# Chunk 0's decays by broadcast from DRAM, the loads reordered, decode 1 to 4 in block 0's first product

## The chip, the cores and the metric

The kernel runs on one core of one Trainium2 chip. The time is device microseconds of that core from one launch; a run's figure is the median of several executions.

## What is computed

Two stages follow each other. The first is a Mamba-2 recurrence over 4 batches and 8 heads (32 pairs), 768 tokens, head size 32 and state size 16. With cum the running sum of log(a) inside a chunk, L[i, j] = exp(cum[i] - cum[j]) for j up to i and zero elsewhere, a chunk gives

```
y     = ((C B^T) * L) x  +  (C state) * exp(cum)
state = exp(cum[last]) * state + sum_j B_j x_j exp(cum[last] - cum[j])
```

The second stage is a dense layer pair on the 3072 x 256 result: h = y @ w_in (256 x 2048), g = h * clip(h + 3, 0, 6) / 6, out = g @ w_out (2048 x 256). The two weights arrive as 64-bit floats; the kernel turns their bits into 32-bit floats itself.

## The kernel before, in words

The reference takes chunks of 32 tokens; the kernel takes chunks of P = 128, so NC = 6 chunks c for each of NB = 4 batches b. Block k of the dense stage holds chunk k of all four batches (512 tokens). The order of all work is written out by hand: each engine runs its instructions in the order in which the program names them, and SP's queue issues its DMAs in that order too.

**Decays.** a is loaded first; clip, Ln and a scan on DVE (lines 192 to 195) give cum for all 32 (b, h) rows. Four DMAs on ScalarE's queue (line 200) write it to DRAM as cum_d. For chunks 1 to 5, `load_decay` (line 205) reads a 4 KB row of cum_d into all 128 partitions (512 KB for each batch), `decay` (line 272) masks it on POOL (for c over 1 it also adds cum_n there) and takes the exponential on ScalarE. `load_eto` (line 212) fetches the rows that scale C for the state term, by eight DMAs. For chunk 0 the kernel builds the differences on TensorE instead: `diff_first` (line 220) puts the mask into a PSUM tile with one matmul and adds each head's row with four more, twice for each batch, and `decay_first` (line 235) takes the exponentials out of PSUM.

**One chunk.** `ends` scales B and, after chunk 0, the old state. `turn` transposes C and B of two batches. `scores` makes C B^T for the heads in four PSUM tiles and multiplies them into L on DVE. `mix` makes y and the state's part; `keep` copies y to yT (ScalarE) and the state (DVE). For chunks from 1 on these pieces come from the generator `steps` (line 426), which yields between them so that they can be set among the dense matmuls of the block before.

**Dense stage.** `mlp_in(k, f)` makes a 128 x 512 tile h for each of 16 values of f (two products of a k half each), then r on ScalarE and gT on DVE. `mlp_out(k, b, f0, f1)` sums over f into the output of batch b. The PSUM pool `ps` has four tiles shared by h, t_ps and cb.

**Weights.** Each weight matrix has four pieces of 1 MB: pieces 0 to 3 are w_in (four f each), 4 to 7 are w_out (four f each). `load_w(i)` loads a piece into one of three raw buffers; `decode_a`, `decode_b`, `decode_c` turn it into fp32. decode_a: the top 16 bits copied on ScalarE; mantissa, exponent and sign cut on DVE; the exponent rebased by a Relu on ScalarE (line 163), with bias bias_e. decode_b: clamp the exponent and add the sign (line 169), join the low mantissa bits (line 171), and start the load of piece i + 3. decode_c: the product (line 185).

**The hand-written order.** Lines 110 to 113 issue w piece 0, chunk 0's C, B and x, then w pieces 1 and 2. Lines 457 to 488 do chunk 0 with decodes 0 and 1 set among its parts, then the loads of chunk 1. From line 491 on a table `weave` spreads decodes 2 to 5 over the 16 f of block 0's first product, three parts in three of four f; decode 6 stands ahead of block 0's second product and decode 7 inside it. `next(todo)` after f 9, after f 13 and later advances the following chunk.

Of the kernel before, what the change touches and what calls it, by code (L numbers as in the profile page):

```python
# [8 lines left out]
FP32 = mybir.dt.float32  # L9
U32 = mybir.dt.uint32  # L10
U16 = mybir.dt.uint16
BF16 = mybir.dt.bfloat16
AF = mybir.ActivationFunctionType
ALU = mybir.AluOpType
# [5 lines left out]
def kernel(  # L20
# [48 lines left out]
    def big(shape, name):  # L69

        return att.tile(shape, FP32, name=name, tag="big", bufs=8)
# [5 lines left out]

    loaded = {}

    def load(c):  # L80
        sl = slice(c * P, (c + 1) * P)
        bc = loads.tile([P, 2, NB * NH, N], FP32, name="bc")
        xt = loads.tile([P, NB * NH, D], FP32, name="xt")
        for j, src in enumerate((C, B)):
            nc.sync.dma_start(  # L85
                out=bc[:, j], in_=src[:, :, sl, :].rearrange("b h s n -> s (b h) n"))
        nc.sync.dma_start(out=xt, in_=x[:, :, sl, :].rearrange("b h s d -> s (b h) d"))
        loaded[c] = bc, xt

    w_in = const.tile([P, NK, DF], FP32, name="w_in")  # L90
    w_out = const.tile([P, NF, DM], FP32, name="w_out")
# [5 lines left out]
    def load_w(i):  # L97
        raw = loads.tile([P, NK * FP * 2 * P], U32, name="raw", bufs=NRAW)
        if i < NP:
            cols = slice(2 * i * FP * P, 2 * (i + 1) * FP * P)  # L100
            src = moe_w_in[:, cols].rearrange("(k p) f -> p k f", p=P)
            dst = raw.rearrange("p (k f) -> p k f", k=NK)
        else:
            r0 = (i - NP) * FP * P
            src = moe_w_out[r0:r0 + FP * P, :].rearrange("(k p) m -> p k m", p=P)
            dst = raw.rearrange("p (k m) -> p k m", k=FP)
        nc.sync.dma_start(out=dst, in_=src)
        raws[i] = raw

    load_w(0)  # L110
    load(0)
    load_w(1)
    load_w(2)
    nc.scalar.preload_act_table_set("natural_log_exp_and_others")


    ident = const.tile([P, P], FP32, name="ident")
    make_identity(nc, ident)
    ident_h = const.tile([P, P], BF16, name="ident_h")
    nc.vector.tensor_copy(ident_h, ident)  # L120
    hide = const.tile([P, P], BF16, name="hide")
    nc.gpsimd.memset(hide, 0.0)
    nc.gpsimd.affine_select(
        out=hide, in_=hide, pattern=[[1, P]], compare_op=ALU.is_ge,
        fill=-1e5, base=0, channel_multiplier=-1)
    run = big([NB * NH, NC, P], "run")
    nc.vector.memset(run, 1.0)
    nc.vector.memset(run[:, :, 0:1], 0.0)
    half = const.tile([P, 1], FP32, name="half")
    nc.vector.memset(half, 0.5)  # L130
    bias_e = const.tile([P, 1], FP32, name="bias_e")
    nc.vector.memset(bias_e, -896.0 * 2 ** 7)
    head = const.tile([P, 2, HU, D], FP32, name="head")
    nc.gpsimd.memset(head, 1.0)
    nc.gpsimd.affine_select(
# [9 lines left out]
    def decode_a(i):  # L145

        n = NK * FP * P
        top = raws[i].bitcast(U16).rearrange("p (n w) -> p n w", w=4)[:, :, 3]  # L150
        hi = raws[i].rearrange("p (n w) -> p n w", w=2)[:, :, 1]
        s = att.tile([P, n], U16, name="ws")
        e = att.tile([P, n], U16, name="we")
        m = att.tile([P, n], U32, name="wm")
        nc.scalar.copy(out=s, in_=top)
        nc.vector.tensor_scalar(
            out=m, in0=hi, scalar1=0xFFFFF, scalar2=0x100000,
            op0=ALU.bitwise_and, op1=ALU.bitwise_or)
        nc.vector.tensor_scalar(  # L159
            out=e, in0=s, scalar1=0x7FF0, scalar2=None, op0=ALU.bitwise_and)  # L160
        nc.vector.tensor_scalar(
            out=s, in0=s, scalar1=0x8000, scalar2=None, op0=ALU.bitwise_and)
        nc.scalar.activation(e.bitcast(BF16), e, AF.Relu, bias=bias_e, scale=8.0)  # L163
        halves[i] = s, e, m

    def decode_b(i):
        s, e, m = halves[i]
        lo = raws.pop(i).rearrange("p (n w) -> p n w", w=2)[:, :, 0]
        nc.vector.scalar_tensor_tensor(
            out=e, in0=e.bitcast(BF16), scalar=255.0 * 2 ** 7, in1=s, op0=ALU.min, op1=ALU.add)  # L170
        nc.vector.scalar_tensor_tensor(
            out=m.bitcast(FP32), in0=lo, scalar=2.0 ** -32, in1=m, op0=ALU.mult, op1=ALU.add)
        if i + NRAW < 2 * NP:
            load_w(i + NRAW)

    def decode_c(i):
# [18 lines left out]
    nc.vector.tensor_tensor_scan(  # L195
        out=flat, data0=run.rearrange("g c p -> g (c p)"), data1=a_sb, initial=0.0,
        op0=ALU.mult, op1=ALU.add)
    cum_d = dram.tile([NB, NC, NH, P], FP32, name="cum_d")
    for b in range(NB):
        nc.scalar.dma_start(  # L200
            out=cum_d[b].rearrange("c h p -> h c p"), in_=cum[b * NH:(b + 1) * NH])

    Ls, etos, diffs = {}, {}, {}

    def load_decay(c, b, queue):
        L = big([P, NH, P], "L")
        src = cum_d[b, c].rearrange("h p -> (h p)").unsqueeze(0)
        queue.dma_start(
            out=L.rearrange("j h i -> j (h i)"), in_=src.to_broadcast([P, NH * P]))
        Ls[c, b] = L  # L210

    def load_eto(c):
        eto = att.tile([P, NB, P], FP32, name="eto")
        for h in range(NH):
            nc.sync.dma_start(  # L215
                out=eto[h * N:(h + 1) * N],
                in_=cum_d[:, c, h].unsqueeze(0).to_broadcast([N, NB, P]))
        etos[c] = eto

    def diff_first(b):  # L220

        rows = NB * NH
        for u in range(2):
            g = b * NH + HU * u
            d = ps_o.tile([P, HU, P], FP32, name="d", tag="o")
            nc.tensor.matmul(
                out=d, lhsT=ident_h, rhs=hide.unsqueeze(1).to_broadcast([P, HU, P]),
                start=True, stop=True)
            for q in range(HU):
                nc.tensor.matmul(  # L230
                    out=d[:, q], lhsT=ident[:rows, g + q:g + q + 1].to_broadcast([rows, P]),
                    rhs=cum[:, 0], start=False, stop=True, skip_group_check=True)
            diffs[b, u] = d

    def decay_first(b):
        Ls[0, b] = big([P, NH, P], "L")
        for u in range(2):
            decay_exp(0, b, diffs.pop((b, u)), HU * u, HU)

    def decay_exp(c, b, src, h0, n):  # L240

# [184 lines left out]
    def steps(c):  # L426

        ends(c)
        turn(c, 0)
        decay(c, 0)  # L430
        yield
        turn(c, 1)
        decay(c, 1)
        yield
        for b in range(NB):
            scores(c, b)
            if c + 1 < NC:
                load_decay(c + 1, b, nc.sync)
            if b + 2 < NB:
                decay(c, b + 2)  # L440
            if b:
                mix(c, b - 1)
            if b == 2:
                keep(c, 0)
            yield
        mix(c, 3)
        keep(c, 1)
        if c + 1 < NC:
            load_eto(c + 1)

    def decode(i):
        decode_a(i)
        decode_b(i)
        decode_c(i)


    decode_a(0)
    by_token()
    diff_first(0)
    turn(0, 0)  # L460
    decay_first(0)
    turn(0, 1)
    decode_b(0)
    decode_c(0)
    ends(0)
    diff_first(1)
    scores(0, 0)
    decay_first(1)
    decode_a(1)
    diff_first(2)  # L470
    scores(0, 1)
    mix(0, 0)
    decay_first(2)
    decode_b(1)
    diff_first(3)
    scores(0, 2)
    mix(0, 1)
    keep(0, 0)
    decay_first(3)
    decode_c(1)  # L480
    scores(0, 3)
    mix(0, 2)
    mix(0, 3)
    keep(0, 1)
    load(1)
    load_eto(1)
    for b in range(NB):
        load_decay(1, b, nc.sync)


    weave = {}
    for i in range(2, 6):
        for j, part in enumerate((decode_a, decode_b, decode_c)):
            weave[0, 4 * (i - 2) + j] = part, i
    for k in range(NC):
        todo = steps(k + 1) if k + 1 < NC else iter(())
        for f in range(NF):
            mlp_in(k, f)
            if (k, f) in weave:
                part, i = weave[k, f]  # L500
                part(i)
            if f in (9, 13):
                next(todo, None)
        if k + 2 < NC:
            load(k + 2)
        next(todo, None)
        if k == 0:
            decode(6)
            for i in range(NP):
                for b in range(2):  # L510
                    mlp_out(0, b, i * FP, (i + 1) * FP)
                if i == 1:
                    decode(7)
                if i != 0:
                    next(todo, None)
        else:
            for b in range(2):
                mlp_out(k, b, 0, NF)
                next(todo, None)
            mlp_out(k, 2, 0, NF // 4)  # L520
            next(todo, None)
            mlp_out(k, 2, NF // 4, NF)
        if k == 0:
            mlp_out(k, 2, 0, NF)
        next(todo, None)
        mlp_out(k, 3, 0, NF)
# [30 lines left out]
```

## Time and profile before

| Quantity | Value |
|---|---|
| Time, median of 3 runs | 457.46 us (456.75 to 457.71) |
| Profiled execution's own time | 457.29 us |
| Span in its profile | 455.6 us |
| PE busy | 425.9 us (93%) |
| DVE busy | 162.1 us (36%) |
| ACT busy | 139.0 us (31%) |
| POOL busy | 66.2 us (15%) |
| Mean granted TensorE clock | 0.984 |
| Data moved by DMA | 30.15 MB |

Busy time is the time in which an engine had an instruction under way. Matmuls are pipelined, so a busy PE is not one at its peak. The chain that ended last is followed back from the last instruction to what released it; a windows view gives the busy time of every engine in a stretch of the span. In a timeline row the first two numbers are start and duration, and the bracket tells the idle time before and who ended it. "issue" stands for time in which nothing that the profile shows was waited for. PE is TensorE's matmuls, PEld its weight loads, DVE VectorE, ACT ScalarE, POOL GpSimd, SP the engine that issues most DMAs.

### The profile page before, as it was taken

The numbers are of one execution on the slowest core, as the hardware profiler recorded it, in microseconds if no ns is written. First come the engines' busy times: TensorE is split into PE (matmuls) and PEld (weight loads), VectorE is DVE, ScalarE is ACT, GpSimd is POOL, SyncE is SP. The second block draws the span as 40 slices with busy tenths as digits, with TensorE's granted clock in tenths as the row PEclk, the third lists the DMA queues.
The fourth block names the chain that finished last, engine by engine and source line by source line (L and its number), as shares of the span: only waits on it lengthen the run. The fifth ranks groups of instructions, "written<-read, shape, count | busy, mean of one in ns | idle before, by whom it ended". The sixth has DMA issues, their size and how long they took to land.

```text
span 455.6 us, 5119 instructions
## 1 busy us (share of the span) xinstructions
PE 425.9 (93%) x2020; PEld 271.7 (60%) x2020; DVE 162.1 (36%) x289; ACT 139.0 (31%) x260; POOL 66.2 (15%) x59
## 2 busy tenths in 40 slices
PE   0899987799999999999899999899999999999997
PEld 0676432377864377854377854387854487744785
DVE  3266587884014432124422124413024512034100
ACT  2352546741024520024510024610035410143200
POOL 2000006000000920000910001923300000000000
PEclk9999998779999999999999999999999999999999
DMA  9928993930266003276013185013100000000000
GB/s 156 230 94 127 113 292 128 150 92 24 72 67 93 1 29 100 66 71 86 0 50 101 47 73 79 0 58 105 31 16 1 1 12 14 14 11 0 0 24 23
DMA packets 87048, 30.15 MB, mean 66 GB/s; under 512 B 75536, under 2 KB 81360, under 8 KB 87024
## 3 DMA queue, kind: packets, MB, share of 16 engines
q1 hardware_dynamic: 86800, 29.73, 34.3%
q8 instruction: 16, 0.26, 0.2%
q10 hardware_dynamic: 224, 0.10, 0.2%
q14 instruction: 8, 0.07, 0.1%
HBM read 26.57 MB, written 3.24 MB: 65 GB/s over the span
## 4 chain that ended last, share of the span: by engine, by line
PE 66%; issue 14%; SPq 5%; DVE 5%; ACT 3%; POOL 3%; DMA 3%; ACTq 0%; POOLq 0%
PE o L417 35%; PE h L403 18%; PE cb L335 3%; SPq L215 3%; PE d L230 3%; PE y L364 2%; DVE gT L409 2%; PE y L358 2%; DMA eto<-cum_d 1%; ACT r L408 1%; POOL L L277 1%; SPq L85 1%; POOL L L278 1%; PE y L370 1%; PE t_ps L313 1%
## 5 line engine op out<-in xcount | busy, mean ns | idle before, releaser
L403 PE MATMUL h<-yT,w_in 128*128 128x512 f32 x384 | 171.2, 602 | 4.9 <-DVE csT L325 3.1
L417 PE MATMUL o<-w_out,gT 128*128 128x256 f32 x768 | 175.2, 386 | 0.0
L417 PEld LDWEIGHTS o<-w_out,gT 128*128 128x128 f32 x768 | 145.7, 192 | 25.2 <-issue 6.0
L403 PEld LDWEIGHTS h<-yT,w_in 128*128 128x128 f32 x384 | 72.7, 193 | 92.3 <-issue 83.7
L409 DVE SCALAR_TENSOR_TENSOR gT<-r,h 128x512 f32<-128x512 f32 x96 | 64.9, 686 | 133.3 <-ACT r L408 133.3
L408 ACT ACTIVATE r<-h,half 128x512 f32<-128x512 f32 x96 | 64.0, 685 | 70.9 <-PE h L403 70.9
L343 DVE TENSOR_TENSOR L<-L,cb 128x256 f32<-128x256 f32 x96 | 34.0, 416 | 78.8 <-PE cb L335 76.1
L422 ACT COPY ob<-o 128x256 f32<-128x256 f32 x24 | 8.9, 372 | 165.8 <-PE o L417 133.1
L277 POOL TENSOR_TENSOR L<-L,cum_n 128x1024 f32<-128x1024 f32 x16 | 30.3, 1895 | 14.9 <-DMA L<-cum_d 14.9
L301 POOL TENSOR_TENSOR tmp<-state,eto 128x512 f32<-128x512 f32 x4 | 4.2, 1046 | 188.1 <-ACT eto L298 188.1
L335 PE MATMUL cb<-cT,bT 32*128 32x256 f32 x192 | 25.1, 474 | 6.2 <-DVE gT L409 4.7
L278 POOL TENSOR_SCALAR_AFFINE_SELECT L<-L 128x1024 f32<-128x1024 f32 x20 | 23.7, 1189 | 1.2
L335 PEld LDWEIGHTS cb<-cT,bT 32*128 32x128 f32 x192 | 11.2, 205 | 17.9 <-DVE gT L409 9.9
L282 ACT ACTIVATE L<-L 128x1024 f32<-128x1024 f32 x16 | 17.0, 1063 | 11.8 <-POOL L L278 11.8
L364 PE MATMUL y<-L,xt 128*32 128x128 f32 x384 | 17.3, 297 | 0.0
L230 PEld LDWEIGHTS d<-cum,ident 32*128 32x128 f32 x64 | 14.2, 323 | 4.5 <-issue 4.5
L230 PE MATMUL d<-cum,ident 32*128 32x128 f32 x64 | 16.6, 436 | 0.0
L385 ACT COPY yT<-y 128x256 f32<-128x256 f32 x24 | 7.8, 375 | 27.6 <-PE y L370 26.0
L388 DVE TENSOR_TENSOR state<-y,mask 128x256 f32<-128x256 f32 x10 | 4.2, 424 | 33.3 <-ACT yT L385 33.3
L163 ACT ACTIVATE we<-we,bias_e 128x1024 bf16<-128x1024 uint16 x8 | 9.2, 1148 | 16.6 <-DVE we L159 16.6
L364 PEld LDWEIGHTS y<-L,xt 128*32 128x32 f32 x384 | 9.8, 115 | 5.0 <-issue 1.3
L292 POOL TENSOR_TENSOR bs<-bc,e_from 128x512 f32<-128x512 f32 x5 | 5.3, 1057 | 52.0 <-DMA bc<-in_B_dram 41.6
(52 smaller groups left out, 159.2 us busy)
## 6 DMA issues: line engine op xcount, KB each, us to landing
L<-cum_d SPq DMA_DIRECT2D x20, 512.0 KB, 6.3
raw<-in_moe_w_in_dram SPq DMA_DIRECT2D x4, 1024.0 KB, 6.4
raw<-in_moe_w_out_dram SPq DMA_DIRECT2D x4, 1024.0 KB, 6.8
xt<-in_x_dram SPq DMA_DIRECT2D x6, 512.0 KB, 8.8
out_dram<-ob SPq DMA_DIRECT2D x24, 128.0 KB, 1.7
bc<-in_C_dram SPq DMA_DIRECT2D x6, 256.0 KB, 6.7
bc<-in_B_dram SPq DMA_DIRECT2D x6, 256.0 KB, 7.6
eto<-cum_d SPq DMA_DIRECT2D x40, 32.0 KB, 2.2
```

The source lines that it names most:

```text
L215: nc.sync.dma_start(out=eto[h * N:(h + 1) * N], in_=cum_d[:, c, h].unsqueeze(0).to_broadcast([N, NB, P]))
L230: nc.tensor.matmul(out=d[:, q], lhsT=ident[:rows, g + q:g + q + 1].to_broadcast([rows, P]), rhs=cum[:, 0], start=False, stop=True, skip_gr ...
L277: nc.gpsimd.tensor_tensor(out=L, in0=L, in1=by_j, op=ALU.add)
L278: nc.gpsimd.affine_select(out=L, in_=L, pattern=[[0, NH], [1, P]], compare_op=ALU.is_ge, fill=-1e5, base=0, channel_multiplier=-1)
L282: nc.scalar.activation(L, L, AF.Exp)
L335: nc.tensor.matmul(out=cb.rearrange("j h i -> j (h i)"), lhsT=bT[rows, b % 2], rhs=cT[rows, b % 2].rearrange("n t i -> n (t i)"), start=Tr ...
L343: nc.vector.tensor_tensor(out=L[:, hs], in0=L[:, hs], in1=cbs[q], op=ALU.mult)
L364: nc.tensor.matmul(out=y_ps[u][32 * q:32 * q + 32, k], lhsT=xt[:, b * NH + h], rhs=L[:, h], start=(c == 0), stop=True, tile_position=(0, 3 ...
L403: nc.tensor.matmul(out=h, lhsT=w_in[:, j, f * P:(f + 1) * P], rhs=yTs[k][:, j].rearrange("p b i -> p (b i)"), start=(j == 0), stop=(j == N ...
L408: nc.scalar.activation(r, h, AF.Relu, bias=half, scale=1.0 / 6.0)
L409: nc.vector.scalar_tensor_tensor(out=gTs[k][:, f], in0=r, scalar=1.0, in1=h, op0=ALU.min, op1=ALU.mult)
L417: nc.tensor.matmul(out=o, lhsT=gTs[k][:, f, b * P:(b + 1) * P], rhs=w_out[:, f], start=(f == 0), stop=(f == NF - 1))
```

## The change

- Chunk 0's decays come from cum_d by the same broadcast DMAs, mask and exponentials as chunk 1's. diff_first, decay_first, ident_h and hide go.
- cum_d gets another layout (chunk, row, token) and is written by one DMA on SP instead of four on ScalarE's queue.
- `load` is split into C and B (`load_bc`) and x (`load_x`). The order on SP at the start is: a, w piece 0, C and B, the write of cum_d, four broadcasts, x, w pieces 1 and 2.
- Chunk 0 runs through `steps(0)` without other work between its parts, behind decode 0. Chunk 1's C, B, x and eto are loaded ahead of it, its broadcasts inside it.
- Decodes 1 to 4, instead of 2 to 5, are woven into block 0's first product; decodes 5, 6, 7 stand inside its second product, one after each quarter but the last.
- In the decode two Relu instructions on ScalarE clamp the exponent at both ends, and DVE joins it with the sign by a bitwise or, instead of one Relu and a min with an add.

```diff
-    load_w(0)
-    load(0)
-    load_w(1)
-    load_w(2)
+    load_w(0)
+    load_bc(0)
...
-    bias_e = const.tile([P, 1], FP32, name="bias_e")
-    nc.vector.memset(bias_e, -896.0 * 2 ** 7)
+    bias_hi = const.tile([P, 1], FP32, name="bias_hi")
+    nc.vector.memset(bias_hi, 1151.0 * 2 ** 7)
+    bias_lo = const.tile([P, 1], FP32, name="bias_lo")
+    nc.vector.memset(bias_lo, 255.0 * 2 ** 7)
...
-        nc.scalar.activation(e.bitcast(BF16), e, AF.Relu, bias=bias_e, scale=8.0)
+        nc.scalar.activation(e.bitcast(BF16), e, AF.Relu, bias=bias_hi, scale=-8.0)
+        nc.scalar.activation(e, e.bitcast(BF16), AF.Relu, bias=bias_lo, scale=-1.0)
...
-        nc.vector.scalar_tensor_tensor(
-            out=e, in0=e.bitcast(BF16), scalar=255.0 * 2 ** 7, in1=s, op0=ALU.min, op1=ALU.add)
+        nc.vector.tensor_tensor(out=e, in0=e, in1=s, op=ALU.bitwise_or)
...
-    cum_d = dram.tile([NB, NC, NH, P], FP32, name="cum_d")
-    for b in range(NB):
-        nc.scalar.dma_start(
-            out=cum_d[b].rearrange("c h p -> h c p"), in_=cum[b * NH:(b + 1) * NH])
+    cum_d = dram.tile([NC, NB * NH, P], FP32, name="cum_d")
+    nc.sync.dma_start(out=cum_d.rearrange("c g p -> g c p"), in_=cum)
...
+    for b in range(NB):
+        load_decay(0, b)
+    load_x(0)
+    load_w(1)
+    load_w(2)
...
         mix(c, 3)
         keep(c, 1)
-        if c + 1 < NC:
+        if 0 < c < NC - 1:
             load_eto(c + 1)
...
     decode_a(0)
     by_token()
-    diff_first(0)
-    turn(0, 0)
-    decay_first(0)
-    turn(0, 1)
     decode_b(0)
     decode_c(0)
-    ends(0)
...
-    decode_a(1)
...
-    keep(0, 1)
     load(1)
     load_eto(1)
-    for b in range(NB):
-        load_decay(1, b, nc.sync)
+    for _ in steps(0):
+        pass
 
 
     weave = {}
-    for i in range(2, 6):
+    for i in range(1, 5):
         for j, part in enumerate((decode_a, decode_b, decode_c)):
-            weave[0, 4 * (i - 2) + j] = part, i
+            weave[0, 4 * (i - 1) + j] = part, i
...
         if k == 0:
-            decode(6)
             for i in range(NP):
                 for b in range(2):
                     mlp_out(0, b, i * FP, (i + 1) * FP)
-                if i == 1:
-                    decode(7)
-                if i != 0:
+                if i + 1 < NP:
+                    decode(NP + i + 1)
                     next(todo, None)
```

More of the change, by code (lines that the diff above doesn't have):

```diff
@@ L78, with load_bc @@
     loaded = {}
-    def load(c):
+    def load_bc(c):
         sl = slice(c * P, (c + 1) * P)
         bc = loads.tile([P, 2, NB * NH, N], FP32, name="bc")
-        xt = loads.tile([P, NB * NH, D], FP32, name="xt")
         for j, src in enumerate((C, B)):
@@ L86, in load, with load_x @@
                 out=bc[:, j], in_=src[:, :, sl, :].rearrange("b h s n -> s (b h) n"))
+        loaded[c] = bc
+    def load_x(c):
+        sl = slice(c * P, (c + 1) * P)
+        xt = loads.tile([P, NB * NH, D], FP32, name="xt")
         nc.sync.dma_start(out=xt, in_=x[:, :, sl, :].rearrange("b h s d -> s (b h) d"))
-        loaded[c] = bc, xt
+        loaded[c] = loaded[c], xt
     w_in = const.tile([P, NK, DF], FP32, name="w_in")
@@ L118 @@
     make_identity(nc, ident)
[L119 to L125, printed above, removed]
     run = big([NB * NH, NC, P], "run")
@@ L197, with load_decay @@
         op0=ALU.mult, op1=ALU.add)
-    cum_d = dram.tile([NB, NC, NH, P], FP32, name="cum_d")
-    for b in range(NB):
-        nc.scalar.dma_start(
-            out=cum_d[b].rearrange("c h p -> h c p"), in_=cum[b * NH:(b + 1) * NH])
-    Ls, etos, diffs = {}, {}, {}
-    def load_decay(c, b, queue):
+    cum_d = dram.tile([NC, NB * NH, P], FP32, name="cum_d")
+    nc.sync.dma_start(out=cum_d.rearrange("c g p -> g c p"), in_=cum)
+    Ls, etos = {}, {}
+    def load_decay(c, b):
         L = big([P, NH, P], "L")
-        src = cum_d[b, c].rearrange("h p -> (h p)").unsqueeze(0)
-        queue.dma_start(
+        src = cum_d[c, b * NH:(b + 1) * NH].rearrange("h p -> (h p)").unsqueeze(0)
+        nc.sync.dma_start(
             out=L.rearrange("j h i -> j (h i)"), in_=src.to_broadcast([P, NH * P]))
@@ L216, in load_eto @@
                 out=eto[h * N:(h + 1) * N],
-                in_=cum_d[:, c, h].unsqueeze(0).to_broadcast([N, NB, P]))
+                in_=cum_d[c, h:NB * NH:NH].unsqueeze(0).to_broadcast([N, NB, P]))
         etos[c] = eto
[L220 to L238, printed above, removed]
+    for b in range(NB):
[3 more added lines that the diff above has]
+    load_w(2)
     def decay_exp(c, b, src, h0, n):
@@ L437, in steps @@
             if c + 1 < NC:
-                load_decay(c + 1, b, nc.sync)
+                load_decay(c + 1, b)
             if b + 2 < NB:
@@ L454, in decode, with load @@
         decode_c(i)
+    def load(c):
+        load_bc(c)
+        load_x(c)
     decode_a(0)
     by_token()
-    diff_first(0)
-    turn(0, 0)
-    decay_first(0)
-    turn(0, 1)
     decode_b(0)
     decode_c(0)
-    ends(0)
-    diff_first(1)
-    scores(0, 0)
-    decay_first(1)
-    decode_a(1)
[L470 to L483, printed above, removed]
-    keep(0, 1)
     load(1)
     load_eto(1)
-    for b in range(NB):
-        load_decay(1, b, nc.sync)
+    for _ in steps(0):
+        pass
     weave = {}
-    for i in range(2, 6):
+    for i in range(1, 5):
         for j, part in enumerate((decode_a, decode_b, decode_c)):
-            weave[0, 4 * (i - 2) + j] = part, i
+            weave[0, 4 * (i - 1) + j] = part, i
     for k in range(NC):
```

## The prediction

> **What bounds the kernel now.** I read the busy time by stage first, because the shares over the whole span mix stages with different limits.
>
> ```profile
> 10.00:20.00 10.00, 7.02 (x30) 5.64 (x31) 2.07 (x4) 2.58 (x4) 1.06 (x1) 1.00 1.20 263
> 20.00:38.00 18.00, 17.35 (x86) 11.68 (x84) 11.34 (x18) 9.29 (x28) 0.00 (x0) 1.00 0.20 66
> 60.00:90.00 30.00, 21.93 (x50) 9.12 (x49) 24.83 (x33) 20.54 (x44) 8.26 (x6) 0.88 0.93 174
> 90.00:130.00 40.00, 40.00 (x252) 30.97 (x253) 16.94 (x32) 8.79 (x20) 0.00 (x0) 0.92 0.22 65
> 130.00:200.00 70.00, 68.56 (x335) 42.85 (x334) 20.32 (x41) 19.05 (x33) 13.90 (x10) 1.00 0.35 60
> ```
>
> Columns after the length: PE, PEld, DVE, ACT, POOL busy, granted clock, DMA share, GB/s. PE fills 14 to 38 (chunk 0's differences) and everything from 91 on. Between 60 and 90 DVE (24.8 of 30 us) and ACT lead. All edits act before 130 us; what follows is PE-bound and unchanged, so a shift at 130 us is a shift of the end. Next the chain that ended last, up to 91 us:
>
> ```profile
> 7.15 2.89 DMA cum_d<-cum
> 10.06 1.10 ACT ws L155
> ...
> 14.37 2.00 PE d L230 x8
> 16.37 0.54 PE d L226
> ...
> 78.02 1.43 DVE w_out L185
> ...
> 91.03 9.68 PE o L417 x32
> ```
>
> The chain runs through the wait of ACT behind the cum_d issues, the difference matmuls, and later the decode on DVE. Last the timeline of block 0's first product, one quarter of it (four of 16 f steps, one decode):
>
> ```profile
> 47.22 15.29 PE L403 MATMUL h<-yT,w_in 128*128 128x512 f32 x35 [0.47 <-ACT yT L385]
> 60.24 1.15 ACT L163 ACTIVATE we<-we,bias_e 128x1024 bf16<-128x1024 uint16 x1 [2.42 <-DVE we L159]
> 62.00 0.69 DVE L409 SCALAR_TENSOR_TENSOR gT<-r,h 128x512 f32<-128x512 f32 x1 [1.33 <-ACT r L408]
> 62.60 1.22 DVE L169 SCALAR_TENSOR_TENSOR we<-we,ws 128x1024 uint16<-128x1024 bf16 x1
> 63.74 1.22 DVE L171 SCALAR_TENSOR_TENSOR wm<-raw,wm 128x1024 f32<-128x1024 uint32 x1
> 64.87 0.68 DVE L409 SCALAR_TENSOR_TENSOR gT<-r,h 128x512 f32<-128x512 f32 x1
> 65.47 1.22 DVE L185 SCALAR_TENSOR_TENSOR w_in<-wm,we 128x1024 f32<-128x1024 f32 x1
> ```
>
> PE runs ahead: for 15 us it never waits, since the weights of f 4 to 7 were decoded before 47.2. gT of f 1 starts at 53.4, of f 5 at 62.0: 8.6 us a quarter, set by DVE plus 1.33 us in which it waits for r behind the Relu.
>
> **What the Trainium skill says.** (1) "DMA: Bandwidth & Descriptors", Queues, rings and completion order: descriptors of one queue are consumed in ring order, and each engine alternates between queues. The trace agrees: cum_d went out on a queue of its own, and its first three pieces, issued 4 us after B, landed at 9.9 to 10.4, ahead of B at 12.7 (the fourth was issued at 9.7, when C had landed, and came at 13.1). (2) "TensorE: Matmul & The Clock Gate", What's actually happening: an array that was idle for a window falls to half its clock, and a busy window brings it back. The trace: granted clock 0.50 from 78 to 82 us, after a PE wait of 3.1 us; and 8 cb matmuls take 1.24 us at 42.5 against 0.71 at 100.6, so the prologue too ran at half speed. (3) "VectorE: DVE Perf Modes", The perf-mode tier table: a 16-bit tensor_tensor in SBUF runs at two elements a cycle. No row of before shows one. (4) "ScalarE: Activation LUTs", What ACT_TABLE_LOAD costs: about 280 ns + 0.833 ns an element with a bias operand, 1.13 us here; the row shows 1.15.
>
> **Step 1, the loads.** Now a, w piece 0, C and B go first, then one cum_d write, the wait for its landing, four 512 KB broadcasts, x, and w pieces 1 and 2. All stand on SP's queue, so x and w wait for the write; before, x was issued at 7.2. The landing records of before: C 9.7, B 12.7, x 16.1, w pieces 18.7 and 21.2. The write is issued at about 7.2 but stands behind B's 64 B pieces: it lands near 12.9 (11 if it could overtake, 13.5 at worst). The four broadcasts of chunk 1 were issued from 54.7 and landed 4.2, 5.8, 8.3 and 10.0 us later; their packets ran from 55.8 for 7.2 us. So chunk 0's land from 17.2 to 23.0, their packets end at 21.3, x takes 3.9 us of packets (as from 10.9 to 14.7 before) and 1.1 to its receipt: 26.3. Pieces 1 and 2 then land near 28.8 and 31.3; the first is used at 40, so they cost nothing.
>
> **Step 2, the start of the first product.** Removed: 8 x (0.54 + 2.0) = 20.3 us of PE, all on the chain; decode 1 (5.2 us of DVE, partly on it); the ACT stall (copy at 10.06, now at 6.6, when w piece 0 is in). The ident_h cast, hide and the memsets (0.06 to 0.29 us each) lie under the wait for a: nothing, at most 0.3 if uncovered. Added: four selects on POOL (1.19 us, up to 2.1 beside DVE), each under the landing of the next broadcast; exps from SBUF, 32 x 0.39 against 0.38. First select at 17.2, exps from 18.4, then ACT at 2.4 us a batch to about 28.4. But PE has its scores 0 and 1, then mix 0, which needs x at 26.3, and scores 2 stand behind it. At the durations of before: mix 0 1.8, scores 2 1.25, mix 1 1.7, scores 3 (beside keep) 1.2, mix 2 1.5, mix 3 1.55, copy and release 0.45: 9.5 us. Start at **36.0 instead of 47.2: -11.2** (32 if the exps set it: the last batch, 2.0 for multiply and mix, 1.55; 39 if x lands at 29). The loads of chunk 1, its eto (8 issues of 0.43 us) and its decays now stand on SP behind w piece 3 and ahead of piece 4: they land by about 56 and are used from 67; piece 4, issued at about 45 instead of 37, lands by 60 and is used at about 79. Hidden.
>
> **Step 3, the first product to the first output matmul** (before 47.2 to 91.0: 43.8). It holds decodes 1 to 4 instead of 2 to 5, as many, but f 4, 8 and 12 now need the piece decoded in the quarter just ended. Per decode: the second Relu +1.05 on the path (r is queued behind it on ACT, gT behind r), between 0 and 1.15; OR 0.69 (estimate from "VectorE: DVE Perf Modes", Side-by-side: 512 cycles plus about 150 at 0.96 GHz; ends 0.55 and 1.22) for 1.22: -0.55. Net +0.5, four times +2.0. New wait: after the decode's last step PE makes h (1.72, since four matmuls of 0.43), then r (0.3 + 0.7), then gT; DVE has only the previous gT (0.7) in that time. Behind that h on PE stand the next tiles and chunk 1's turn and scores. 2.7 - 0.7 = 2.0 a deadline, three deadlines 6.0, and 1.0 for what moves with it at f 9 (eto's exp, selects and eight exps: gT 9 to gT 10 is 6.7 us already, and the last decode step is behind it). PE now idles over 4 us a quarter, so half clock: +0.85 for a cold first tile (half of 1.7) and +2.0 for about one of three deadlines met cold (each 1.7; 0 to 5). Sum +11.85, a product of 55.6: the first output matmul at **91.6 instead of 91.0: +0.6**.
>
> **Step 4, the second product** (before 91.0 to 129.6, PE without a pause). Before, output pieces 0 and 1 were ready at its start and 2 and 3 by 97 and 103. Now piece 0 only; decodes 5, 6, 7 follow inside, in DVE's and ACT's order between the scores of chunk 1. One decode alone, with its waits for ACT: 0.7 + 0.4 + 2.3 + 0.7 + 1.1 + 1.2 = 6.4 us; the scores' four multiplies between decodes 1.4, and keep's two 0.8 once. DVE is free 0.8 after the start, so the pieces are ready at 7.2, 15.0 and 23.6. PE has per quarter 16 matmuls (3.55, the first, cold, 4.8) and a step of scores and mix (2.0), so it asks at 6.8, 12.75 and 20.55: waits 0.4 + 2.25 + 3.05 = 5.7. Before lost 2.6 to the half clock here (9.68 for 32 matmuls, later 7.10); only the first 16 are cold now: -1.3. **+4.4** (2 to 6).
>
> **Sum.** -11.2 + 11.8 + 4.4 = +5.0 against the profiled execution's 457.3 (span 455.6 and 1.7 around it), which lies 0.2 under the median of 457.5: **462.3 us**.
>
> **The rivals.** *A, as above*, 459 to 467: chance 0.62. *B, faster*: the deadlines at f 4, 8 and 12 cost little, because PE holds four h tiles and DVE finds work in them. Then only +2.0 stands in the first product: 457.3 - 11.2 + 2.0 + 4.4 = 452.5. It decides when the three waits, cold tiles included, sum to less than 4.8 us, 1.6 each. For it: DVE's waits of 1.33 are the largest in a quarter today. Against: PE must see the last decode step first, and only one gT is queued then. 0.13. *C, the clock*: PE at 60% duty stays at half clock through the first product; four h at 3.43 make 13.7 us a quarter against 11.3, the start of the outputs comes at about 97.5, and 1.5 is lost in the second product: 457.3 + 6.5 + 4.4 + 1.5 = 469.7. For it: 0.50 was granted after 3 us of waiting; against: it recovered within 7 us under load. 0.15. *D, balance*: x lands 3 to 4 us earlier than worked out, or the OR and warm tiles save it, and the sum is nil, within 0.2% (0.9 us, about what a measurement here can tell from no change): 0.10.
>
> **Range.** Slower 0.62 + 0.15 = 0.77, same 0.10, faster 0.13. OR at 1.22 would add up to 3.8, x at either end -5 to +3. From 455 (leaves out most of B, 0.09) to 469 (leaves out about 0.10 of C).
>
> **What would show it.** Right: no L230 on the chain, the first h near 36, PE waiting for w_in L185 before f 4, 8, 12 with 11 to 12 us between them, first output matmul at 90 to 93, PE waits for w_out L185 in the second product. Wrong: mix waiting on L rather than x; first output matmul before 87 (B) or after 96 (C); no PE wait behind 91 us.

## The result and the profile after

| | before | after |
|---|---|---|
| Median of 4 runs, us | 457.48 (456.75 to 457.71) | 462.94 (460.47 to 464.05) |
| Ratio to before, with 95% interval | | 1.0115 [1.0070, 1.0159] |
| Profiled execution, its span, us | 457.29, 455.6 | 462.30, 460.6 |
| Mean granted TensorE clock | 0.984 | 0.967 |
| First h matmul of block 0, us | 47.2 | 31.7 |
| First output matmul, us | 91.0 | 90.4 |
| First h matmul of block 1, us | 129.5 | 134.5 |

The kernel became slower by about 5 us. It starts the dense stage 15.6 us earlier, and loses 20.6 us between there and the start of block 1. (The prediction has 129.6 for before, from the chain; the first matmul record stands at 129.45.) Behind that point the two kernels take 326 us each.

A quarter below is the four f that use one piece of w_in, and a deadline is the first f of a quarter, which must wait until its piece is decoded. The windows view of after, cut at the moments when PE goes on after such a wait (columns: stretch, length, then PE, PEld, DVE, ACT, POOL busy, granted clock, DMA share, GB/s):

```profile
31.60:44.00 12.40, 7.13 (x16) 2.96 (x16) 7.47 (x11) 6.03 (x9) 1.15 (x1) 0.95 0.82 140
44.00:57.40 13.40, 9.85 (x16) 4.02 (x16) 6.86 (x12) 5.83 (x7) 0.00 (x0) 0.75 0.56 193
57.40:74.90 17.50, 10.45 (x20) 4.43 (x20) 9.89 (x13) 8.93 (x17) 6.68 (x5) 0.70 0.30 110
74.90:90.40 15.50, 12.63 (x28) 5.49 (x28) 8.96 (x16) 10.93 (x25) 0.00 (x0) 0.83 0.18 54
90.40:134.40 44.00, 39.39 (x249) 30.80 (x249) 19.52 (x37) 14.46 (x24) 1.37 (x1) 0.92 0.43 94
```

In the quarter from 44.0 no engine is busy throughout: PE 9.9 of 13.4 us, DVE 6.9, ACT 5.8. Before, DVE led this stage at 24.8 of 30 us. Here three engines take turns. The waits view of PE names the turn (us in total, times, longest):

```profile
PE h L384 <- DVE w_in L182: 15.8, 3, 7.1
...
PE o L398 <- DVE w_out L182: 4.6, 2, 2.8
```

The timeline of after shows one such turn:

```profile
42.81 1.22 DVE L182 SCALAR_TENSOR_TENSOR w_in<-wm,we 128x1024 f32<-128x1024 f32 x1
...
44.08 9.85 PE L384 MATMUL h<-yT,w_in 128*128 128x512 f32 x16 [5.28 <-DVE w_in L182]
...
47.90 0.69 ACT L389 ACTIVATE r<-h,half 128x512 f32<-128x512 f32 x1 [6.91 <-PE h L384]
48.48 1.10 ACT L152 COPY ws<-raw 128x1024 uint16<-128x1024 uint16 x1
...
48.62 0.69 DVE L390 SCALAR_TENSOR_TENSOR gT<-r,h 128x512 f32<-128x512 f32 x1 [4.00 <-ACT r L389]
...
50.28 1.15 ACT L160 ACTIVATE we<-we,bias_hi 128x1024 bf16<-128x1024 uint16 x1 [0.69 <-DVE we L156]
...
51.46 1.15 ACT L161 ACTIVATE we<-we,bias_lo 128x1024 uint16<-128x1024 bf16 x1
...
53.22 0.69 DVE L390 SCALAR_TENSOR_TENSOR gT<-r,h 128x512 f32<-128x512 f32 x1 [2.51 <-ACT r L389]
53.82 0.69 DVE L167 TENSOR_TENSOR we<-we,ws 128x1024 uint16<-128x1024 uint16 x1
```

The last step of decode 1 (L182) ends at 44.0, and only then can PE make h of f 4. r follows it on ACT, gT follows r, and the first step of decode 2 (L152) stands on ACT behind that r: the next decode can't begin before the tile that waited for this one is through. The ring closes once per quarter, and it runs cold (at half clock): the clock records of after give 0.5 in 42.8 to 49.6, 56.4 to 63.2 and 70.1 to 80.3, so each of the three tiles after a wait is made at half clock. The chain that ended last shows the third turn, cold h (3.79 us for four matmuls) included:

```profile
72.16 0.58 ACT r L389
72.76 0.69 DVE gT L390
73.45 1.44 DVE w_in L182
74.94 3.79 PE h L384 x4
78.75 0.70 ACT r L389
```

L230, the difference matmuls, is gone from it. The timeline of after at the start shows what the first h now hangs on:

```profile
7.37 2.27 SPq L196 DMA_DIRECT2D cum_d<-cum  x1
...
11.18 1.77 SPq L203 DMA_DIRECT2D L<-cum_d  x4
...
15.32 1.23 PE L316 MATMUL cb<-cT,bT 32*128 32x256 f32 x6 [2.78 <-DVE cT L300]
...
15.71 2.33 POOL L259 TENSOR_SCALAR_AFFINE_SELECT L<-L 128x1024 f32<-128x1024 f32 x2 [3.39 <-DMA L<-cum_d]
16.83 2.44 ACT L225 ACTIVATE L<-L,cum_n 128x128 f32<-128x128 f32 x8 [4.74 <-POOL L L259]
...
19.18 0.35 ACT L298 COPY bT<-t_ps 128x256 f32<-128x256 f32 x1
...
19.57 0.69 DVE L300 TENSOR_TENSOR cT<-t_ps,parity 128x512 f32<-128x512 f32 x1 [4.30 <-ACT bT L298]
...
20.31 2.95 PE L316 MATMUL cb<-cT,bT 32*128 32x256 f32 x10 [3.77 <-DVE cT L300]
...
23.19 1.08 PE L345 MATMUL y<-L,xt 128*32 128x128 f32 x16
```

The landing records give B at 10.95 us, cum_d at 11.16, the four broadcasts at 15.64, 16.88, 18.53 and 19.89, x at 22.19, the w pieces at 25.66 and 28.16. mix 0 (L345) begins at 23.19, right behind scores 1; nothing waits for x. What PE waited for at 20.31 is the second turn's cT, which waits for bT, which stands on ACT behind the eight exponentials of the first broadcast. Six of batch 0's eight cb products had run at 15.32; by the order of the four `ps` tiles the last two go into the one that this cT has to read first. From 20.31 to 31.2 PE is busy for 10.88 of 10.89 us.

### The profile page after: what moved, and what is told of

Read it like the earlier page. It is cut to its first block, busy times and chain, and to the rows that moved or that the text cites. A ratio compares the mean times of both kernels' runs of the same rounds, so it can differ in the third digit from the quotient of the medians.

```text
span 460.6 us, 4992 instructions
## 1 busy us (share of the span) xinstructions
PE 413.2 (90%) x1948; PEld 260.1 (56%) x1948; DVE 159.4 (35%) x289; ACT 149.5 (32%) x268; POOL 70.1 (15%) x61
## 4 chain that ended last, share of the span: by engine, by line
PE 58%; issue 18%; DVE 6%; SPq 6%; ACT 5%; POOL 3%; DMA 3%; POOLq 0%; ACTq 0%
PE o L398 32%; PE h L384 19%; SPq L210 3%; PE cb L316 2%; SPq L84 2%; DMA bc<-in_B_dram 2%; PE y L345 2%; DVE gT L390 2%; ACT r L389 1%; PE y L339 1%; ACT L L225 1%; POOL L L259 1%; DMA eto<-cum_d 1%; POOL L L258 1%; ACT we L160 1%
## 5 line engine op out<-in xcount | busy, mean ns | idle before, releaser
L384 PE MATMUL h<-yT,w_in 128*128 128x512 f32 x384 | 176.9, 618 | 16.3 <-DVE w_in L182 15.8
L384 PEld LDWEIGHTS h<-yT,w_in 128*128 128x128 f32 x384 | 74.9, 198 | 107.6 <-issue 84.4
L316 PE MATMUL cb<-cT,bT 32*128 32x256 f32 x192 | 25.6, 473 | 12.8 <-DVE cT L300 6.5
L259 POOL TENSOR_SCALAR_AFFINE_SELECT L<-L 128x1024 f32<-128x1024 f32 x24 | 27.5, 1152 | 5.5 <-DMA L<-cum_d 4.2
L316 PEld LDWEIGHTS cb<-cT,bT 32*128 32x128 f32 x192 | 11.8, 203 | 26.2 <-DVE gT L390 10.5
L225 ACT ACTIVATE L<-L,cum_n 128x128 f32<-128x128 f32 x64 | 19.3, 389 | 7.1 <-POOL L L259 7.1
L263 ACT ACTIVATE L<-L 128x1024 f32<-128x1024 f32 x16 | 17.0, 1062 | 11.8 <-POOL L L259 11.8
L345 PE MATMUL y<-L,xt 128*32 128x128 f32 x384 | 16.7, 292 | 0.0
L366 ACT COPY yT<-y 128x256 f32<-128x256 f32 x24 | 7.8, 375 | 15.9 <-PE y L351 14.4
L160 ACT ACTIVATE we<-we,bias_hi 128x1024 bf16<-128x1024 uint16 x8 | 9.2, 1148 | 10.2 <-DVE we L156 10.2
L345 PEld LDWEIGHTS y<-L,xt 128*32 128x32 f32 x384 | 9.6, 114 | 4.8 <-issue 1.9
L168 DVE SCALAR_TENSOR_TENSOR wm<-raw,wm 128x1024 f32<-128x1024 uint32 x8 | 11.5, 1437 | 0.0
```

Source lines behind the costliest of these rows:

```text
L225: nc.scalar.activation(Ls[c, b][:, h0 + q], src[:, q], AF.Exp, bias=cum_n[:, c, g:g + 1])
L259: nc.gpsimd.affine_select(out=L, in_=L, pattern=[[0, NH], [1, P]], compare_op=ALU.is_ge, fill=-1e5, base=0, channel_multiplier=-1)
L263: nc.scalar.activation(L, L, AF.Exp)
L316: nc.tensor.matmul(out=cb.rearrange("j h i -> j (h i)"), lhsT=bT[rows, b % 2], rhs=cT[rows, b % 2].rearrange("n t i -> n (t i)"), start=Tr ...
L345: nc.tensor.matmul(out=y_ps[u][32 * q:32 * q + 32, k], lhsT=xt[:, b * NH + h], rhs=L[:, h], start=(c == 0), stop=True, tile_position=(0, 3 ...
L384: nc.tensor.matmul(out=h, lhsT=w_in[:, j, f * P:(f + 1) * P], rhs=yTs[k][:, j].rearrange("p b i -> p (b i)"), start=(j == 0), stop=(j == N ...
```

## The experiments

Two of the kernels (the warm ones) add matmuls whose result nothing reads; none leaves anything out. Ratios are to the kernel before, run beside them on the same chip, in three groups (its medians 456.70, 456.74 and 457.25 us).

**The new order of the decodes alone.** The kernel before keeps its difference matmuls and its decode; only decode 1 to 4 are woven into the first product, and 5 to 7 into the second.

```diff
-    decode_a(1)
...
-    decode_b(1)
...
-    decode_c(1)
...
-    for i in range(2, 6):
+    for i in range(1, 5):
...
-            decode(6)
...
-                if i == 1:
-                    decode(7)
-                if i != 0:
+                if i + 1 < NP:
+                    decode(NP + i + 1)
```

> The kernel before (chunk 0's differences on TensorE, its loads, its decode) with the decodes placed as after: 1 to 4 in the first product, 5 to 7 in the second. Theory of deadlines: first h at 45 to 47, a first product of 55 to 58 us instead of 43.8, a second of 42 to 44 instead of 38.6: 469 to 476 us. Rival, the placement of the decodes costs nothing by itself: 456 to 459 us. Rival, only the second product loses: 461 to 463 us.

Measured: 472.05 us, 1.0340 [1.0286, 1.0395]. The waits of PE in this kernel:

```profile
PE h L403 <- DVE w_in L185: 14.0, 3, 7.5
...
PE o L417 <- DVE w_out L185: 2.4, 2, 2.2
```

First h at 47.3 as before; the first product takes 55.6 instead of 43.8 us, the second 42.8 instead of 38.5. So the order by itself costs 15 to 16 us, with no part of the other edits in it.

**The same edit taken back in the kernel after.** decode 1 goes ahead of the first product again; broadcasts and the two Relus stay.

```diff
     for _ in steps(0):
         pass
+    decode(1)
...
-    for i in range(1, 5):
+    for i in range(2, 6):
...
+            decode(6)
...
-                if i + 1 < NP:
-                    decode(NP + i + 1)
+                if i == 1:
+                    decode(7)
+                if i != 0:
```

> The kernel after, but decode 1 stands whole behind chunk 0 and ahead of the first product, decodes 2 to 5 are woven as in the kernel before, 6 ahead of and 7 inside the second product. Theory of deadlines (what the earlier start wins is lost because the first product waits at f 4, 8 and 12 for the piece just decoded, and the second product for pieces 5 to 7): first h still near 31.7, no wait of PE for w_in, first gT near 39 instead of 34.4 since decode 1 stands ahead of it, first output matmul near 82 instead of 90.4, second product 39 to 40 us instead of 44: 446 to 453 us. Rival, the decode's form costs (a second Relu in each of eight decodes): as many Relus as after, so 460 to 463. Rival, the loads: unchanged order, so 460 to 463.

Measured: 450.09 us, 0.9865 [0.9820, 0.9910]. Two lines of its timeline, gT of f 1 and of f 5:

```profile
43.90 0.69 DVE L390 SCALAR_TENSOR_TENSOR gT<-r,h 128x512 f32<-128x512 f32 x1 [2.51 <-ACT r L389]
...
53.16 0.69 DVE L390 SCALAR_TENSOR_TENSOR gT<-r,h 128x512 f32<-128x512 f32 x1 [2.51 <-ACT r L389]
```

A quarter is 9.26 us, though the decode is that of after and the first h (32.2) nearly so; there the quarter was 13.35. PE has no wait for w_in left, and the second product is back at 38.8 us. The two experiments agree from both ends: the deadlines, at f 4, 8 and 12 and for pieces 5 to 7 inside the second product, eat the earlier start.

**The form of the decode.** In after, the decode of before is put back (one Relu; min and add on DVE instead of the or).

```diff
-    bias_hi = const.tile([P, 1], FP32, name="bias_hi")
-    nc.vector.memset(bias_hi, 1151.0 * 2 ** 7)
-    bias_lo = const.tile([P, 1], FP32, name="bias_lo")
-    nc.vector.memset(bias_lo, 255.0 * 2 ** 7)
+    bias_e = const.tile([P, 1], FP32, name="bias_e")
+    nc.vector.memset(bias_e, -896.0 * 2 ** 7)
...
-        nc.scalar.activation(e.bitcast(BF16), e, AF.Relu, bias=bias_hi, scale=-8.0)
-        nc.scalar.activation(e, e.bitcast(BF16), AF.Relu, bias=bias_lo, scale=-1.0)
+        nc.scalar.activation(e.bitcast(BF16), e, AF.Relu, bias=bias_e, scale=8.0)
...
-        nc.vector.tensor_tensor(out=e, in0=e, in1=s, op=ALU.bitwise_or)
+        nc.vector.scalar_tensor_tensor(
+            out=e, in0=e.bitcast(BF16), scalar=255.0 * 2 ** 7, in1=s, op0=ALU.min, op1=ALU.add)
```

> The kernel after with the decode of the kernel before: one Relu, then min and add instead of two Relus and a bitwise or. Theory of deadlines: each decode on the path gains a Relu (1.15) and loses 0.5 on DVE, so about 0.6 for each of four in the first product and three in the second, less where a half-clock window sets the time: 458 to 461 us, and the waits of PE for w_in stay over 12 us. Rival, the decode's form is what the change costs: 457 us or less, the waits of PE mostly gone.

Measured: 457.33 us, 1.0021 [1.0002, 1.0041], a time between theory and rival. The waits of PE decide for the theory, since they stay:

```profile
PE h L382 <- DVE w_in L180: 13.9, 3, 7.5
```

The quarter from f 4 to f 8 is 12.71 instead of 13.35 us, the first product 55.7 instead of 58.8, the second 42.9 instead of 44.0, while the first h comes at 32.5 instead of 31.7. So with the old form the deadlines alone bring the kernel back to about the time of before, and most of what after loses against it (1.0115, and 1.0105 repeated) is the new form. The opposite edit, the two Relus and the or put into the kernel before:

> The kernel before with the two-Relu decode alone. Theory: each decode in the first product's DVE chain costs 1.15 of ScalarE less 0.55 of DVE, four of them 2.4 to 2.6 us, the prologue's and the second product's are hidden: 459 to 461 us. Rival, without deadlines ScalarE's second Relu is hidden behind PE's lead of four tiles: 456 to 458 us.

Measured: 459.28 us, 1.0047 [1.0033, 1.0061]; its quarter is 9.26 instead of 8.6. So the new form costs about 0.65 us in a quarter of either order. In before its first product grows by 3.3 us (47.0 against 43.7) while the first h comes 1.1 earlier (46.15), which sums to about the 2.1 that the ratio shows. DVE is relieved by 1.22 - 0.68 = 0.54, but it isn't the one waited for: its wait for r grows from 1.33 to 2.51, since r stands on ACT behind the second Relu.

**Both edits taken back** (decode 1 ahead and the old form, so that of the change the broadcasts, the single write and the order of the loads are left):

> The kernel with decode 1 ahead of the first product, now with the one-Relu decode of the kernel before as well. Theory of deadlines with the Relu priced as measured in the deadlines' quarters (0.64 us each): about 0.6 for each of five decodes ahead of the first output, none in the second product, which PE fills: 446 to 448 us, quarters of 8.6 instead of 9.3 us. Rival, without deadlines the Relu is hidden: 449 to 451.

Measured: 446.16 us, 0.9758 [0.9740, 0.9776]. That is what the broadcast part is worth with decode 1 ahead of the product. The first h comes 15.2 us earlier than in before (32.0), of which 3.7 go at once: the first gT stands 6.5 us behind it instead of 2.7, since decode 1 is now ahead of it on DVE.

**The clock.** Unread matmuls fill PE's wait ahead of f 4, 8 and 12, so that h is made warm; the deadlines stay.

```diff
+    FILL = {4: 5, 8: 5, 12: 7}
...
+            if k == 0 and f in FILL:
+                if f == min(FILL):
+                    z = ps_o.tile([P, TB], FP32, name="z", tag="o")
+                for _ in range(FILL[f]):
+                    nc.tensor.matmul(
+                        out=z, lhsT=w_in[:, 0, :P],
+                        rhs=yTs[0][:, 0].rearrange("p b i -> p (b i)"), start=True, stop=True)
             mlp_in(k, f)
```

> The kernel after with matmuls added whose result nothing reads, 5, 5 and 7 of 128x512 on TensorE ahead of f 4, 8 and 12, where PE waits; they keep the array busy and nothing else. Theory that the granted clock falls to half in each of the three waits and costs 1.7 us of the first tile after each: clock 1.0 from 44 to 75, gT 2.7 instead of 4.5 us after the piece is ready, 457 to 460 us. Rival, the clock is hidden because DVE sets the pace of a quarter: 462 to 464 us. Rival, the added matmuls get in the way of h: over 464 us.

Measured: 456.31 us, 1.0002 [0.9976, 1.0029]. The windows view of this kernel for two of the stretches shown above:

```profile
44.00:57.40 13.40, 13.28 (x31) 5.70 (x31) 7.14 (x11) 5.78 (x8) 0.00 (x0) 1.00 0.63 228
57.40:74.90 17.50, 15.38 (x41) 6.85 (x40) 11.01 (x14) 10.64 (x19) 6.67 (x5) 1.00 0.22 78
```

and its timeline:

```profile
43.78 7.13 PE L384 MATMUL h<-yT,w_in 128*128 128x512 f32 x16 [0.98 <-DVE w_in L182]
...
46.53 0.69 DVE L390 SCALAR_TENSOR_TENSOR gT<-r,h 128x512 f32<-128x512 f32 x1 [2.20 <-ACT r L389]
...
50.76 4.45 PE L464 MATMUL z<-yT,w_in 128*128 128x512 f32 x10
55.34 3.70 PE L384 MATMUL h<-yT,w_in 128*128 128x512 f32 x8
```

The clock column reads 1.00 instead of 0.75 and 0.70. gT of f 4 comes 2.75 us after PE goes on instead of 4.54, and the quarter is 11.56 instead of 13.35 us: 1.8 us of this quarter were the cold tile, since the other work and its order are the same. The same with the old form of the decode:

> The kernel after with both the one-Relu decode and the added matmuls (4, 4 and 7, read by nothing) ahead of f 4, 8 and 12. Theory that the half clock (about 5.4 us) and the second Relu (0.64 us a quarter, and its share of the second product) add up: quarters of 10.9 us instead of 13.3, 452 to 454 us, and what still lies between this and the kernel with decode 1 ahead of the product is the wait itself, 2 us a deadline. Rival, they hide one another: 456 to 457 us.

Measured: 453.94 us, 0.9924 [0.9903, 0.9945], quarter 10.91. Form and clock add up. From here to 446.16 it is still 0.9924 - 0.9758 = 1.7%, 7.6 us. In the profiles 0.8 of it lies ahead of the first h, 3.1 in the first product (50.9 against 47.8) and 3.6 in the second (41.1 against 37.5). The clock doesn't explain the first product's part: it is 0.5 for 2.8 us there, and for 7.0 in the faster kernel.

**The start.** cum_d goes out in the new layout, by four DMAs on ScalarE's queue as in before; the rest is after.

```diff
-    nc.sync.dma_start(out=cum_d.rearrange("c g p -> g c p"), in_=cum)
+    for b in range(NB):
+        gs = slice(b * NH, (b + 1) * NH)
+        nc.scalar.dma_start(out=cum_d[:, gs].rearrange("c h p -> h c p"), in_=cum[gs])
```

> The kernel after, but cum_d is written by four DMAs on ScalarE's queue as in the kernel before (in the new layout). Theory that pieces on a second queue share the engines with B's 64-byte pieces and slow both: B lands near 12.5 instead of 10.95, the first broadcast is issued near 12.5 to 13.5 instead of 11.2, ScalarE's copy of w piece 0 waits for the fourth issue until about 10, first h 1.5 to 2.5 us later, 464 to 466 us. Rival, the single write on SP is what holds the broadcasts, since it stands behind B: cum_d lands by 10.4 and the first h comes up to 1 us earlier, 461 to 463 us.

Measured: 459.83 us, 1.0052 [1.0035, 1.0069], below what both said. Its timeline at the start:

```profile
6.30 1.67 ACTq L198 DMA_DIRECT2D cum_d<-cum  x4
...
8.86 2.20 SPq L205 DMA_DIRECT2D L<-cum_d  x4
```

The four pieces land at 8.85 to 10.19, so SP issues the broadcasts at 8.86 and not at 11.18; the first lands at 13.68 instead of 15.64, and the first h comes at 29.8 instead of 31.7. B stayed at 10.96: my theory that the second queue would hold B up fell. The other direction, x moved ahead of the write of cum_d:

```diff
     load_bc(0)
+    load_x(0)
...
-    load_x(0)
     load_w(1)
```

> The kernel after with x loaded right behind C and B, ahead of the write of cum_d and the broadcasts. Theory that B's last pieces land late when x's pieces follow them at once (12.7 in the kernel before, 10.95 after): B lands near 12.5, cum_d behind x near 15, broadcasts from 15 on, the exponentials set the first h at 34 to 36 instead of 31.7, x no longer waited for: 464 to 467 us. Rival, the step from 12.7 to 10.95 came from ScalarE's queue: B at 11 here too, and cum_d at 14.

Measured: 464.54 us, 1.0148 [1.0112, 1.0185]. x is in at 14.1 instead of 22.2 and it helps nothing: the broadcasts are issued at 14.4 and the first h comes at 34.4. Over these kernels the first broadcast landed at 13.7, 15.6 and 18.6 and the first h stood at 29.8, 31.7 and 34.4. The first h follows the first broadcast by 15.9 to 16.1 us; it doesn't follow x.

**Towards a better kernel.** decode 1 ahead with the old form, but its first part set inside chunk 0, so that ACT and DVE have less to do before the first gT:

```diff
-    for _ in steps(0):
-        pass
-    decode(1)
+    for n, _ in enumerate(steps(0)):
+        if n == 4:
+            decode_a(1)
+    decode_b(1)
+    decode_c(1)
```

> As the last one, but decode_a(1) stands between scores 2 and scores 3 of chunk 0, where ScalarE has done its exponentials, and only decode_b and decode_c behind chunk 0, while DVE waits for the first h. Expected: the first gT near 36 instead of 38, first h up to 1.5 us later, together 1 to 2 us less than the last one: 444 to 447 us. Rival: multiply and keep of chunk 0 are held up by as much as the decode gains: no difference, 446 to 448 us.

Measured: 445.47 us, 0.9743 [0.9728, 0.9757]. This interval overlaps that of the unsplit one, so nothing is decided on the split. Last, this kernel with the four DMAs of cum_d on ScalarE's queue:

> The kernel with decode 1 split ahead of the first product and the one-Relu decode, now with cum_d written by four DMAs on ScalarE's queue. Theory that one write on SP, standing behind B and read by all four broadcasts, holds their start by 2.3 us (11.2 against 8.9): first h near 31.9 instead of 33.8, 443 to 445 us. Rival, the first gT is set by decode 1 there and not by the first h: no difference, 445 to 446.

Measured: 443.38 us, 0.9697 [0.9682, 0.9713], the fastest of all, 3% under the kernel before. Its timeline:

```profile
77.67 8.75 PE L398 MATMUL o<-w_out,gT 128*128 128x256 f32 x32
...
115.16 17.33 PE L384 MATMUL h<-yT,w_in 128*128 128x512 f32 x40
```

The first output matmul comes at 77.7 and block 1's first h at 115.2, where after has 90.4 and 134.5.

**After once more**, as the measure for small differences:

> The kernel after itself, unchanged, beside the others on the same chip. Every theory: 460 to 464 us, ratio 1.008 to 1.015 to the kernel before.

Measured: 461.72 us, 1.0105 [1.0069, 1.0140]. Its first h is at 30.8, its first product 57.9 us.

## Why the prediction was right, and where it was not

The time (462.3 predicted, 462.94 median and 462.30 profiled) and the case (A) were right. That the sum came so close is luck: its terms were off by 4.4, 3.2 and 1.1 us, the first against the other two, and cancelled:

| Step | Predicted, us | Measured, us |
|---|---|---|
| First h | 36.0 (-11.2) | 31.7 (-15.6) |
| First product | 55.6 (+11.8) | 58.8 (+15.0) |
| Second product | 38.6 + 4.4 = 43.0 | 44.0 (+5.5) |
| Sum | +5.0 | +5.0 |

**Step 1** held in its order but was some 2 us pessimistic: it took B at 12.7 from the trace of before, with the write of cum_d at 12.9 behind it, and B came at 10.95 and the write at 11.16. The broadcasts and x then came 1.6 to 4.1 us earlier than worked out. The decode's edit goes with that (see what stays open); the prediction priced that edit among the decodes alone. That the write stands behind B was right, and moving it off SP's queue was worth 1.9 us of first h in one profile each (1.0 against the repeat of after) and 0.5% by the ratios (1.0052 against 1.0105, whose intervals touch).

**Step 2** failed in its cause: "mix 0, which needs x at 26.3". x was in at 22.2, and with x at 14.1 the start became later. Its own sign for this, mix waiting on L rather than x, came only in part: mix 0 began at 23.19 without a wait. The case it put in brackets, "32 if the exps set it", has the measured number but not its cause: the exponentials end at 26.6, not 28.4, and the first h comes 5.1 us behind them, not 3.55. What sets it is PE's own row of scores and mixes, at work without a pause from 20.31 on. What the prediction lacked is that ACT runs the first batch's exponentials ahead of the copy of bT, so that the second turn's cT waits for the first broadcast, and with it the last of batch 0's cb products and every multiply into L.

**Step 3** had the mechanism right (r and gT behind the deadline, four h tiles no help, the second Relu on the path) and the sizes low. "About one of three deadlines met cold" failed: all three were, while the very first tile was warm. The warm kernel separates the terms, once a delay that it shares with after is taken out. In both profiles one DVE instruction of decode 1 took 1.28 us instead of 0.42 (after repeated has the 0.42); in after:

```profile
35.46 1.15 POOL L273 TENSOR_TENSOR bs<-bc,e_from 128x512 f32<-128x512 f32 x1 [14.41 <-DMA bc<-in_B_dram]
35.61 1.28 DVE L156 TENSOR_SCALAR we<-ws 128x1024 uint16<-128x1024 uint16 x1
```

Without this 0.9 the warm first product is 53.0 us (half clock in its last 2.3 alone), where the sum without new cold tiles (43.8 + 2.0 + 6.0 + 1.0) says 52.8: the waits and the form together were sized within 0.2. After, repeated, takes 57.9, so cold tiles cost 4.9 instead of 0.85 + 2.0. 0.2 + 2.0 + 0.9 = 3.1 is the miss: the clock above all. The form of the decode was priced at +2.0 in this product: 57.9 against 55.7 gives 2.2. It is 0.65 to 0.75 for each decode whose piece PE waits for, and 0.1 in the last quarter, where nobody does.

**Step 4** had the pieces ready 7.2, 15.0 and 23.6 us after the start; the timeline has 7.1, 14.8 and 23.4. PE waited 1.8 + 2.8 = 4.6 instead of 5.7, but the clock fell to 0.5 for 3.4 us again (114.4 to 117.9). "Only the first 16 are cold now" was what failed; the stage is 1.0 longer than predicted.

**The rivals.** B (faster) was to decide when the three waits cost under 1.6 us each, cold tile included; the quarter grew by 4.1 (13.35 against the 9.26 of the kernel with decode 1 ahead), 1.8 of it the cold tile. C (half clock throughout) was half true: the granted clock was 0.75, 0.70 and 0.83 in the last three quarters, neither warm nor steadily cold, because 16 matmuls in a row brought it back and the next wait took it away. "TensorE: Matmul & The Clock Gate" of the Trainium skill, What's actually happening, speaks of a window of 3.4 us; the clock records of after agree: up to the end of the second product each stretch at 0.5 lasted one, two or three times 3.41 us.

**What stays open.** In the seven profiles with the two Relus (after and its repeat, and kernels of both orders) C lands at 8.6 to 9.0 us and B at 10.9 to 11.1; in the seven with one Relu, before among them, C at 9.7 to 10.2 and B at 12.1 to 12.8. Neither x behind B nor the second queue makes the difference. The packet records show it in the small packets themselves, over the whole run: one of 64 bytes (C and B) took 10.9 to 11.0 ns on average in the first seven and 13.6 to 14.6 in the others, one of 128 bytes (x) 13.0 against 20.0 to 23.2, while packets of 2048 bytes took 88 to 101 in both. One candidate fits all fourteen: the new form has one constant more, each constant takes 32 bytes of a partition, and the load buffers lie behind them, so that in the programs bc begins at a multiple of 64 bytes (77568 in after) in the first seven kernels and 32 off one (78048 in before) in the others. No kernel that only shifts the buffers was run, so this is argued, not shown; nor was the fastest kernel, which has the old form, run with such a shift. It also means that every exchange of the decode's form above holds this change of the loads. The 1.28 us of DVE's L156 occur in three of the fourteen profiles, and in just these three POOL's bs was under way when L156 began; L156 ended 0.28 us after bs each time. That DVE waits for POOL there is likely, but no run moved the one away from the other.

## What to carry to other kernels

Work that makes operands for a later stage should run one stage ahead: if, as here, a piece is finished in the quarter in which it is first needed, the consumer's own tail (here h, r, gT) joins the producer's chain, and the busy shares won't show it: look for a stretch in which no engine leads. Count such a wait on PE with the half clock that followed it here, each time. To shorten an instruction on one engine at the price of a longer one on another, look first which of the two is waited for: here DVE gave back 0.54 us per decode and waited 1.18 longer.

## What the hardware showed

- Around a PE wait of 3.5 to 7.1 us, in quarters in which PE was 60 to 81% busy, the granted clock was 0.5 for 6.8 to 10.2 us. 17 unread 128 x 512 products (two matmul rows of 0.43 to 0.45 us each) held it at 1.0 from 28 to 83 us and brought the ratio from 1.0105 to 1.0002.
- An or of two 128 x 1024 16-bit tensors took 0.68 us on DVE (the estimate from "VectorE: DVE Perf Modes" of the Trainium skill, Side-by-side, was 0.69), and min with add of the same size 1.22.
- C and B, in 64-byte pieces, landed 0.7 to 1.9 us earlier in one set of kernels than in another that loads them with the same instructions (above).
- The clock records of before begin at 45.0 us and those of after at 29.1; ahead of that a windows view reads 1.00 for want of a record. Eight cb products took 1.24 us at 42.5 in before and 0.71 at 100.6, so a 1.00 there doesn't mean full speed.
